# Fused top-k attention and two MoE layers on one core: keys and queries turned plain and stacked by DMA, last two batches in two visits

## Chip, cores and metric

The kernel runs on one core of a Trainium2 chip. The time is device time in microseconds (us) of the whole program, from inputs in HBM to outputs in HBM. The engines are PE (TensorE), VectorE (DVE), ScalarE (ACT), GpSimd (POOL) and SP, which in this kernel issues the DMAs.

## What is computed

Three layers follow each other; the output of one is the input of the next.

```python
# attention: B, H, S, D = 4, 8, 576, 64
scores = q @ k.T / 8
kth = np.partition(scores, -32, axis=-1)[..., -32:-31]
attn = softmax(where(scores >= kth, scores, -1e9))
x = (attn @ v)                      # -> 2304 tokens x 512
# first MoE
x = ((x @ w1) * (x @ w2)) @ w3 @ w_out
# second MoE: 8 experts, w1 512 x 1024, w2 1024 x 512
P = exp(x @ w_gate - max); 8 times: divide by row sums, by column sums, scale
out = sum over e of P[:, e:e+1] * (maximum(x @ w1[e], 0) @ w2[e])
```

## The kernel before

**Attention.** A *visit* is one batch and one pair of heads (`visits`, line 92). Two visits make a group of nine *steps* (`steps1`, line 220): four steps with 128 query rows of both heads of the first visit, one step for the 64 rows that are left over of both visits, four steps of the second visit. There are 72 steps. In a step `st_scores` multiplies queries with keys (L251), `st_topk` finds the 32nd largest score on VectorE with rounds of max and replace (L300, L305), `st_over`, `st_exp` and `st_norm` make the weights, `st_trans` turns them (L360, L361) and `st_av` multiplies them with the values (L389). Three steps are in work at once: scores for step s + 1, top-k of s, weights of s - 1, values of s - 2. A string in `ORDERS` (three of them: for steps below `SWITCH`, for the other steps with weight conversion, and for the rest) tells in which order a step's pieces are issued: S scores, T the maxima that feed top-k, f and d top-k, O and E weights, N normalising, R turning, A values, P a piece of preparation, C a weight conversion, F filling, X handing over a batch.

Scores have fp32 accuracy from two fp32r halves: a key is kept as high and low half, stacked over 128 partitions, and in a second tile with the halves swapped (`kst[p, 0]`, `kst[p, 1]`); queries are stacked likewise in `qst_t`. `prep_list(p)` makes these for visit p: `prep_split` (ScalarE copies the high half, GpSimd subtracts), `prep_group` (PE turns blocks of both halves side by side, L174, ScalarE copies them out, L133), and `prep_swap` (two DMAs make the swapped tile, L207). The loop over p (from L745) spreads these pieces over steps. `load_pair` and `load_v` fetch keys, queries and values; all DMAs are issued by SP, in the order of the program.

**First MoE.** While batch 0 is in attention, weights are converted (`convert`, `cv_run`) and w3 @ w_out is folded into `W` (L538). A batch's products become *filling* when its last step is done (`pdone`, `marks`): `moe1_list` gives, for a part of 256 or 320 tokens, `x_split`, 32 pieces of `ab` (six matmuls each, L588) and 16 of `x2_mm` (L606), and the gate's logits (`gate_parts`, `gate_sums`). `run_fill` takes pieces of it from the list `fill` up to a budget `per`, which deals what is left evenly over the steps to the last mark. The last batch's filling runs after attention.

**Second MoE.** Three thirds of the tokens, eight experts, four pieces of the hidden layer make 96 *units*. `l1` multiplies x with the first weights in seven products (L1005), `l2` multiplies the result with the second (L1066) and adds it up on VectorE (L1079). Seven places a unit call `slot()`, which takes one entry of the list `steps`: x of the next third is loaded, summed (VectorE, L921), and split (ScalarE L924, GpSimd L927) there by `x_ops`. `w_split` and `w2_split` split weights on ScalarE and GpSimd (L893, L894, L901, L902).

Of the kernel before, what the change touches and what calls it, by code (L numbers as in the profile page):

```python
# [7 lines left out]
F32 = mybir.dt.float32  # L8
# [10 lines left out]
def kernel(  # L19
# [45 lines left out]
    nc.sync.dma_start(wg[:, :, 0:E], w_gate.rearrange("(c p) e -> p c e", p=128))  # L65
# [25 lines left out]
    SPLIT = {}  # L91
# [15 lines left out]

    def load_pair(p):
        b, hp, (t0, t1), tail = visits[p]
        for nm, src, r0, r1, end in (("k", k, 0, R, True), ("q", q, t0, t1, tail)):  # L110
            t = ap1.tile([128, 2 * R + 1, D], F32, name=f"{nm}n", tag=f"{nm}n", bufs=1)
            nc.sync.dma_start(
                t[:, 0:2 * R].rearrange("p (h r) d -> p h (r d)", h=2)[:, :, D * r0:D * r1],
                src[b, 2 * hp:2 * hp + 2, 0:S4, :].rearrange("h (p r) d -> p h (r d)", r=R)[:, :, D * r0:D * r1])
            for i in range(2 if end else 0):
                nc.sync.dma_start(t[64 * i:64 * i + 64, 2 * R], src[b, 2 * hp + i, S4:S, :])
            nat[nm, p] = t

# [18 lines left out]
    def prep_split(p, nm, eng=nc.gpsimd, three=False):  # L137
        src = nat.pop((nm, p))
        if three:
            hl = xT[0].rearrange("p c s -> p (c s)")[:, 0:3 * S].rearrange("p (n a d) -> p n a d", a=3, d=D).bitcast(F32R)  # L140
        else:
            hl = ap1.tile([128, 2 * R + 1, 2, D], F32R, name=f"{nm}hl", tag=f"{nm}hl")
        (t0, t1), tail = visits[p][2:]
        if nm == "k" or t1 - t0 == R:
            parts = [(src, hl[:, :, 0, :], hl[:, :, 1, :])]
        else:
            hr = hl[:, 0:2 * R].rearrange("p (h r) a d -> p h r a d", h=2)[:, :, t0:t1]
            parts = [(src[:, 0:2 * R].rearrange("p (h r) d -> p h r d", h=2)[:, :, t0:t1], hr[:, :, :, 0], hr[:, :, :, 1])]
            if tail:
                parts.append((src[:, 2 * R], hl[:, 2 * R, 0], hl[:, 2 * R, 1]))  # L150
        for x, hi, lo in parts:
            nc.scalar.activation(hi, x, AF.Copy)
            eng.tensor_tensor(lo, x, hi.bitcast(F32), ALU.subtract)
        if three:
            nc.scalar.activation(hl[:, :, 2, :], src, AF.Copy)
        split[nm, p] = hl

    def qgroups(p):
        (t0, t1), tail = visits[p][2:]
        n = t1 - t0  # L160
        heads = [[R * h + t for t in range(t0, t1)] for h in range(2)]
        r = heads if n > 2 else [heads[0] + heads[1]]
        if tail:
            r = r[:-1] + [r[-1] + [2 * R]] if n == 1 else r + [[2 * R]]
        return r

    def prep_group(p, nm, g, eng=None, flip=False):
# [22 lines left out]
        else:  # L190
            n = int(flip)
            if (p, n) not in kst:
                kst[p, n] = ap1.tile([128, 2, S], F32R, name=f"kst{n}", tag=f"kst{n}", bufs=2)
# [8 lines left out]
    def prep_swap(p, hs=slice(0, 2), ts=slice(0, S)):  # L202

        if (p, 1) not in kst:
            kst[p, 1] = ap1.tile([128, 2, S], F32R, name="kst1", tag="kst1", bufs=2)
        for i in range(2):
            nc.sync.dma_start(kst[p, 1][64 * i:64 * i + 64, hs, ts].bitcast(F32),  # L207
                              kst[p, 0][64 - 64 * i:128 - 64 * i, hs, ts].bitcast(F32))

    def prep_list(p):  # L210
        ops = [lambda: prep_split(p, "k"), lambda: prep_split(p, "q")]
        for nm in ("k", "q"):
            for g in kgroups if nm == "k" else qgroups(p):
                ops.append(lambda nm=nm, g=g: prep_group(p, nm, g))
            if nm == "k":
                ops.append(lambda: prep_swap(p))
        return ops
# [129 lines left out]
    def st_eps(st):  # L347
        nc.gpsimd.tensor_scalar(rden[st], rden[st], 1e-9, None, op0=ALU.add)
# [125 lines left out]
    def cv_list():  # L474
# [14 lines left out]
        def add3(i, hf):  # L489
            add(("3", i, hf), w3[128 * i:128 * i + 128, CW * hf:CW * hf + CW], lambda: w3dst(i, hf),  # L490
                lambda: later(4, w_items(i, hf)))
# [67 lines left out]
    def x_split(b, hf):  # L559
# [4 lines left out]
        eng, step = (nc.vector, 1) if b == B - 1 else (nc.gpsimd, KD)  # L564
# [8 lines left out]
    def ab(b, hf, f, which, part):  # L573
# [7 lines left out]
        for c in (2 * part, 2 * part + 1):  # L581
# [5 lines left out]
            for j, (lhs, rhs) in enumerate(((wh, xh), (wh, xl), (wl, xh))):  # L587
                nc.tensor.matmul(ps[:, 0:n], lhs, rhs[:, c, 0:n],  # L588
                                 start=(c == 0 and j == 0), stop=(c == KD - 1 and j == 2))
# [40 lines left out]
    def gate_sums(b, hf):  # L630
# [548 lines left out]
```

## Time and profile before

| | us |
|---|---|
| median of 3 runs | 2362.26 (2357.11 to 2362.8) |
| the profiled execution, its own time | 2360.21 |
| its span in the profile | 2358.4 |
| PE busy | 2257.2 (96%) |
| VectorE busy | 1874.8 (79%) |
| GpSimd busy | 1563.2 (66%) |
| ScalarE busy | 1262.4 (54%) |

The span is what the profile shows from the first instruction to the last; the 1.8 us around it belong to the time. PE's busy time counts matmuls that overlap, so a busy PE need not be full. Engines are busy by turns, so the shares have to be read by stage. In the profile's names L251 is line 251 of the kernel, and `kst<-pt` is an instruction that reads tile pt and writes kst.

### The profile page before, as it was taken

How to read it: one execution, taken by the hardware profiler on the slowest of the kernel's cores; microseconds unless marked ns; L12 is line 12 of the kernel's file. 1: busy time of each engine (PE TensorE's matmuls, PEld its weight loads, DVE VectorE, ACT ScalarE, POOL GpSimd, SP SyncE). 2: the span in 40 equal slices, each digit the busy share in tenths (PEclk: the TensorE clock that was granted, in tenths of full speed). 3: DMA queues.
4: the chain of work that ended last, by engine and by line, in shares of the span. 5: the costliest groups of instructions: out<-in, count | busy, mean ns of one | idle time of the engine just before them, and what ended most of it. 6: DMA issues, size and time to landing. Idle time of an engine off the chain costs nothing.

```text
span 2358.4 us, 38935 instructions
## 1 busy us (share of the span) xinstructions
PE 2257.2 (96%) x13108; PEld 1990.3 (84%) x13108; DVE 1874.8 (79%) x4352; ACT 1262.4 (54%) x2763; POOL 1563.2 (66%) x1727
## 2 busy tenths in 40 slices
PE   4797899999999999999999999999999999999999
PEld 4554888897997989899999988899998999999998
DVE  7899999999994378887777777777777677777776
ACT  7899788787874344443343453344434434344432
POOL 5789876776763156866666677666666666666664
PEclk7898899999999999999999999999999999999999
DMA  4433111111101022222222232222222222222221
GB/s 149 125 115 116 26 46 53 34 43 53 31 21 44 29 69 85 76 70 66 72 64 72 86 94 68 67 67 68 71 65 68 94 72 63 72 63 72 68 67 54
DMA packets 171704, 161.34 MB, mean 68 GB/s; under 512 B 21360, under 2 KB 136048, under 8 KB 171504
## 3 DMA queue, kind: packets, MB, share of 16 engines
q1 hardware_dynamic: 171504, 158.86, 22.8%
q8 instruction: 103, 1.69, 0.3%
q14 instruction: 97, 0.79, 0.1%
HBM read 140.53 MB, written 9.44 MB: 64 GB/s over the span
## 4 chain that ended last, share of the span: by engine, by line
PE 83%; DVE 5%; ACT 5%; POOL 4%; issue 1%; DMA 1%; SPq 0%; POOLq 0%; ACTq 0%; DVEq 0%
PE y L1066 33%; PE l1ps L1005 29%; PE abps L588 8%; PE x2ps L606 4%; PE sps L251 3%; PE tx L389 2%; PE tx L360 2%; DVE tkv L300 2%; DVE rest L305 1%; PE pt L174 1%; ACT s_sb L341 1%; ACT et L363 1%; POOL xl L568 1%; PE wps L538 1%; ACT xT L446 0%
## 5 line engine op out<-in xcount | busy, mean ns | idle before, releaser
L894 POOL TENSOR_TENSOR wal<-ws,wah 128x256 fp32r<-128x256 f32 x665 | 546.6, 830 | 476.3 <-ACT wah L893 468.7
L1079 DVE SCALAR_TENSOR_TENSOR acc<-y,P,acc 128x512 f32<-128x512 f32 x540 | 402.3, 745 | 205.2 <-PE y L1066 203.5
L893 ACT ACTIVATE wah<-ws 128x256 fp32r<-128x256 f32 x672 | 276.7, 413 | 516.4 <-PE l1ps L1005 510.9
L1066 PE MATMUL y<-wbh,hh 128*128 128x512 f32 x1152 | 454.3, 394 | 5.4 <-ACT hh L1026 5.3
L1066 PE MATMUL y<-wbl,hh 128*128 128x512 f32 x1152 | 455.5, 395 | 0.0
L1066 PE MATMUL y<-wbh,hl 128*128 128x512 f32 x1152 | 452.6, 393 | 1.6 <-DVE hl L1029 1.2
L887 DVE TENSOR_TENSOR ws<-ws 128x256 f32<-128x256 f32 x384 | 327.7, 854 | 0.1
L1005 PE MATMUL l1ps<-xo0h,wah 128*128 128x384 f32 x896 | 303.1, 338 | 0.0
L1005 PE MATMUL l1ps<-xo0l,wah 128*128 128x384 f32 x896 | 301.6, 337 | 0.0
L1005 PE MATMUL l1ps<-xo0h,wal 128*128 128x384 f32 x896 | 301.4, 336 | 0.0
L1026 ACT ACTIVATE hh<-u 128x384 fp32r<-128x384 f32 x192 | 100.9, 526 | 296.9 <-DVE u L1018 296.9
L1066 PEld LDWEIGHTS y<-wbl,hh 128*128 128x128 f32 x1152 | 216.8, 188 | 48.9
L1066 PEld LDWEIGHTS y<-wbh,hh 128*128 128x128 f32 x1152 | 216.8, 188 | 32.3 <-ACT hh L1026 7.7
L1066 PEld LDWEIGHTS y<-wbh,hl 128*128 128x128 f32 x1152 | 216.9, 188 | 30.0 <-DVE hl L1029 4.8
L902 POOL TENSOR_TENSOR wbl<-ws,wbh 128x1024 fp32r<-128x1024 f32 x96 | 232.0, 2416 | 11.9 <-ACT wbh L901 2.8
L277 POOL TENSOR_TENSOR low<-s_sb 128x288 int32<-128x288 int32 x144 | 118.9, 825 | 111.5 <-ACT s_sb L255 108.9
L1005 PEld LDWEIGHTS l1ps<-xo0l,wah 128*128 128x128 f32 x896 | 168.6, 188 | 17.1
L1005 PEld LDWEIGHTS l1ps<-xo0h,wah 128*128 128x128 f32 x896 | 168.4, 188 | 14.5
L300 DVE MAX8 tkv<-rest 128x8 f32<-128x288 f32 x432 | 174.7, 445 | 0.0
L1005 PEld LDWEIGHTS l1ps<-xo0h,wal 128*128 128x128 f32 x896 | 168.4, 188 | 0.0
L1018 DVE TENSOR_TENSOR u<-l1ps,u 128x384 f32<-128x384 f32 x288 | 157.0, 545 | 4.3 <-PE l1ps L1005 2.5
L251 PE MATMUL sps<-kst,qst 128*128 128x288 f32 x640 | 132.7, 336 | 28.5 <-DVE top L284 28.4
(166 smaller groups left out, 5219.8 us busy)
## 6 DMA issues: line engine op xcount, KB each, us to landing
ws<-in_moe_w_dram SPq DMA_DIRECT2D x384, 128.0 KB, 2.3
ws<-in_moe_w_dram SPq DMA_DIRECT2D x96, 512.0 KB, 3.5
raw<-in_moe_w_dram SPq DMA_DIRECT2D x32, 512.0 KB, 3.9
kst<-kst SPq DMA_DIRECT2D x30, 288.0 KB, 4.1
xr<-x2s SPq DMA_DIRECT2D x12, 384.0 KB, 3.8
kn<-in_k_dram SPq DMA_DIRECT2D x16, 256.0 KB, 3.2
qn<-in_q_dram SPq DMA_DIRECT2D x16, 256.0 KB, 3.0
raw<-in_moe_w_out_dram SPq DMA_DIRECT2D x8, 512.0 KB, 4.3
```

Source lines behind the costliest of these rows:

```text
L251: nc.tensor.matmul(ps[:, e, 0:SH], lhs, kst[p, part][:, hh, SH * e:SH * e + SH], start=(n == 0), stop=(n == len(terms) - 1))
L277: nc.gpsimd.tensor_tensor(low_sb[st][:, j].bitcast(I32), x[:, 0:SH], x[:, SH:S], ALU.add)
L300: nc.vector.max(vt[:, j, c:c + 8], x[:, j])
L588: nc.tensor.matmul(ps[:, 0:n], lhs, rhs[:, c, 0:n], start=(c == 0 and j == 0), stop=(c == KD - 1 and j == 2))
L887: nc.vector.tensor_tensor(st[:, dst], st[:, x], st[:, y], op)
L893: nc.scalar.activation(hi, st[:, slot], AF.Copy)
L894: eng.tensor_tensor(lo, st[:, slot], hi.bitcast(F32), ALU.subtract)
L902: nc.gpsimd.tensor_tensor(lo, st, hi.bitcast(F32), ALU.subtract)
L1005: nc.tensor.matmul(ps[:, 0:TH], lhs[:, c], rhs[:, slot, c], start=(k_ == 0), stop=(k_ == 3 * KH - 1))
L1018: nc.vector.tensor_tensor(t[nm], ps, t[x], ALU.add)
L1066: nc.tensor.matmul(ps, lhs[:, m, h, o:o + 128], rhs[:, m], start=(k_ == 0), stop=(k_ == 5))
L1079: nc.vector.scalar_tensor_tensor(a, ps, P[:, t, e:e + 1], a, op0=ALU.mult, op1=ALU.add)
```

## The change

- **Preparation of keys and queries.** They are loaded so that both heads' 64 columns lie side by side, turned once in fp32 (`prep_turn`, four transposes; the left-over rows of keys and queries share one, `prep_ends`), copied out by ScalarE, split after that (`prep_parts`, ScalarE and GpSimd), and the halves are stacked into `kst` and `qst_t` by six and four to eight DMAs (`prep_stack`). The old three functions are gone but for the first visit.
- **Two visits for the last two batches.** `SPLIT` makes each pair of heads of batches 2 and 3 come twice, first with query rows 0 to 255, then with the rest; keys are loaded and prepared for both. There are 24 visits for 16; the number of steps stays 72. A batch's first 256 tokens become filling after its first four visits.
- **Dealing.** `per` is also held to what lasts until the next mark.
- **First loads.** `load_first` puts the first queries on ScalarE's queue, `split_first` splits in pieces, the gate's weights are loaded later, the first scores come before the second head is prepared.
- **Issue orders** in `ORDERS`; one more conversion may wait (`len(dve_q) > 3`), w3's products come two ticks later; `x_split` works in chunks of two; the first product piece reads low halves last; the gate's copies wait in `held`.
- **Second MoE.** The first two products of the first unit (`first_ps`) are issued before the last gate piece. For later thirds, x's four sums take a place each, and places 3 and 4 of a unit call no `slot()` from the seventh unit on.

```diff
-    SPLIT = {}
+    SPLIT = {B - 2: 2, B - 1: 2}
...
+    def prep_turn(p, nm):
+        src = nat.pop((nm, p))
...
+        for t in range(c0 // 128, c1 // 128):
+            nc.tensor.transpose(pt[:, 128 * t:128 * t + 128], src[:, t].rearrange("p h d -> p (h d)"), ident)
+        copy(flat_x[nm, p].bitcast(F32)[:, 1, c0:c1], pt[:, c0:c1], None, scale if nm == "q" else 1.0)
...
+    def prep_parts(p, nm):
...
+        nc.scalar.activation(hi, lo.bitcast(F32), AF.Copy)
+        nc.gpsimd.tensor_tensor(lo, lo.bitcast(F32), hi.bitcast(F32), ALU.subtract)
+
+    def prep_stack(p, nm):
...
+            for h in range(2):
+                x = hl[64 * h:64 * h + 64]
+                nc.sync.dma_start(ks.bitcast(F32)[0:64, :, h], x)
+                for a in range(2):
+                    nc.sync.dma_start(ks.bitcast(F32)[64:128, 1 - a, h], x[:, a])
+            return
+        for h in range(2):
+            for a in range(2):
...
+                nc.sync.dma_start(d[:, S4 * h + c0:S4 * h + cb], x[:, c0:cb])
+                if c1 == S:
+                    nc.sync.dma_start(d[:, 2 * S4 + 192 * h:2 * S4 + 192 * h + 64], x[:, S4:S])
...
-        eng, step = (nc.vector, 1) if b == B - 1 else (nc.gpsimd, KD)
+        eng, step = (nc.vector, 1) if b == B - 1 else (nc.gpsimd, 2)
...
-        "X C N F f0 O0 S0 d0 P f1 d1 T0 R0 O1 B F R1 f2 d2 f3 L F g0 C C P F P C C E0 F V e0 F E1 Q g1 S1 A C F F J T1",
+        "F f0 N P S0 C d0 R0 X P O0 f1 d1 T0 F O1 B R1 F L f2 d2 f3 g0 C C P E0 F C F V C P C F S1 e0 E1 g1 Q C J T1 A F",
...
+            have = todo[0] - sum(work[m] for m in marks[:-1] if m >= s)
+            for m in marks[:-1]:
+                if m >= s:
+                    per = min(per, have / (m + 1.5 - s) / 4)
+                    have += work[m]
...
-            steps += [lambda c=c: sums(c), None]
             if s == 0:
+                steps += [lambda c=c: sums(c), None]
...
+                steps += [lambda c=c, n=n: sums(c, n) for n in range(4)] + [None]
...
+        if len(fill) == 1:
+            for x in order[:2]:
+                first_ps[x] = l1_prod(0, 0, 0, x)
...
-            slot()
+            if n < 6 or i not in (3, 4):
+                slot()
```

Three places show what moves. The first is PE's order from the last weighted values of attention on; abps is the first MoE's first product, x2ps its second, lgps the gate. Before:

```order
L361 MATMUL tx<-ident,s_sb 128x128
L389 MATMUL tx<-et,vn_96 64x128 x10
L606 MATMUL x2ps<-G,W 128x320 x4
L588 MATMUL abps<-xh,w1h 128x256
L588 MATMUL abps<-xl,w1h 128x256
L588 MATMUL abps<-xh,w1l 128x256
L588 MATMUL abps<-xh,w1h 128x256
L588 MATMUL abps<-xl,w1h 128x256
L588 MATMUL abps<-xh,w1l 128x256
L625 MATMUL lgps<-x2st,wg 32x320 x4
```

and with the change:

```order
L398 MATMUL tx<-ident,s_sb 128x128
L426 MATMUL tx<-et,vn_95 64x128 x10
L644 MATMUL x2ps<-G,W 128x256 x8
L627 MATMUL abps<-xh,w1h 128x320 x4
L627 MATMUL abps<-xh,w1l 128x320 x2
L663 MATMUL lgps<-x2st,wg 32x256 x4
L627 MATMUL abps<-xh,w1l 128x320 x2
L627 MATMUL abps<-xl,w1h 128x320 x4
L674 MATMUL lgps<-fold,x2st 128x8 x2
```

Before, both parts of the last batch stand behind this place, the 256-column one first; now it is the 320-column part alone.

The second is SP's order in batch 2, where a visit is half as long as before; vn are values, ends the left-over rows, x2s the first MoE's result. Before:

```order
L207 DMA kst_4904<-kst_4743 64x1152 x2
L613 DMA x2s<-x2st 128x256
L615 DMA x2s<-x2st 128x64
L123 DMA vn_96<-in_v_dram 128x256 x2
L126 DMA vn_96<-in_v_dram 64x64 x2
L112 DMA kn<-in_k_dram 128x2x256
L116 DMA kn<-in_k_dram 64x64 x2
L112 DMA qn<-in_q_dram 128x2x256
L116 DMA qn<-in_q_dram 64x64 x2
L207 DMA kst_5607<-kst_5377 64x1152 x2
```

and with the change, for one visit with query rows 0 to 255:

```order
L134 DMA vn_94<-in_v_dram 128x256 x2
L137 DMA vn_94<-in_v_dram 64x64 x2
L248 DMA qst_97<-qt 64x256 x4
L124 DMA kn<-in_k_dram 128x4x64 x2
L126 DMA ends<-in_k_dram 64x2x64
L124 DMA qn<-in_q_dram 128x2x64 x2
L126 DMA ends<-in_q_dram 64x2x64
L240 DMA kst<-kt 64x2x576
L242 DMA kst<-kt 64x576 x2
L240 DMA kst<-kt 64x2x576
L242 DMA kst<-kt 64x576 x2
L134 DMA vn_95<-in_v_dram 128x256 x2
```

One pair of swap copies between two visits' loads has become six copies of keys and four of queries; the queries' copies stand behind the next load of values.

The third is GpSimd's order in the second MoE while x of the next third is prepared; wbl is the split of the second weights, xo1l the low half of x, u and p sums that the hidden layer waits for. Before:

```order
L1023 TENSOR_TENSOR u_11596<-u_11572,p_11549 128x384
L894 TENSOR_TENSOR wal_11607<-ws_11360,wah_11606 128x256
L902 TENSOR_TENSOR wbl<-ws_11437,wbh 128x1024
L927 TENSOR_TENSOR xo1l<-xr,xo1h 128x384
L894 TENSOR_TENSOR wal_11639<-ws_11360,wah_11638 128x256
L927 TENSOR_TENSOR xo1l<-xr,xo1h 128x384
L1023 TENSOR_TENSOR p_11549<-u_11626,p_11549 128x384
L894 TENSOR_TENSOR wal_11663<-ws_11360,wah_11662 128x256
L894 TENSOR_TENSOR wal_11693<-ws_11360,wah_11692 128x256
```

and with the change:

```order
L1084 TENSOR_TENSOR u_12061<-u_12037,p_12014 128x384
L948 TENSOR_TENSOR wal_12072<-ws_11830,wah_12071 128x256
L956 TENSOR_TENSOR wbl<-ws_11906,wbh 128x1024
L948 TENSOR_TENSOR wal_12102<-ws_11830,wah_12101 128x256
L1084 TENSOR_TENSOR p_12014<-u_12089,p_12014 128x384
L948 TENSOR_TENSOR wal_12124<-ws_11830,wah_12123 128x256
L982 TENSOR_TENSOR xo1l<-xr,xo1h 128x384
L948 TENSOR_TENSOR wal_12153<-ws_11830,wah_12152 128x256
L982 TENSOR_TENSOR xo1l<-xr,xo1h 128x384
```

Two low halves of x stood between the split of the second weights and p; now none does.

## Rows read from the trace of the kernel before

**Rows 1.** Busy time by stretch: busy us (instructions) of PE, PEld, DVE, ACT, POOL; PEclk, DMA, GB/s.

```profile
63.30:248.70 185.40, 148.47 (x920) 100.36 (x921) 170.72 (x562) 175.37 (x358) 153.53 (x181) 0.90 0.37 112
248.70:414.50 165.80, 161.72 (x1338) 146.04 (x1339) 159.78 (x597) 132.56 (x298) 119.02 (x172) 0.97 0.16 43
414.50:721.60 307.10, 299.06 (x2507) 269.43 (x2505) 293.94 (x1097) 241.60 (x540) 215.28 (x312) 0.98 0.13 35
...
745.60:834.50 88.90, 87.75 (x553) 78.09 (x553) 20.72 (x39) 26.87 (x61) 15.31 (x17) 1.00 0.16 46
...
1009.70:1337.30 327.60, 327.60 (x1640) 295.59 (x1639) 258.90 (x402) 132.32 (x294) 213.57 (x210) 1.00 0.23 68
```

**Rows 2.** Chain of waits, attention steps paced by VectorE: start us, us, what.

```profile
700.17 1.44 DVE tkv L300 x4
...
709.02 1.44 DVE tkv L300 x4
```

**Rows 3.** Chain of waits, one attention step from 352.29 to 361.14.

```profile
352.29 1.24 PE tx L389 x20
353.53 0.73 PE sps L251 x4
...
355.13 0.44 PE pt L174 x4
...
356.44 0.44 PE tx L360 x4
...
357.87 0.53 PE sps L251 x4
...
361.14 1.24 PE tx L389 x20
```

**Rows 4.** Chain of waits, from the end of attention to the second MoE.

```profile
749.40 21.79 PE abps L588 x180
...
785.01 0.87 PE abps L588 x6
...
787.87 26.50 PE abps L588 x180
814.37 17.23 PE x2ps L606 x64
...
834.53 2.28 PE l1ps L1005 x12
```

**Rows 5.** ScalarE by line and shape, 63.3 to 248.7 us: count | busy us, mean ns | idle before.

```profile
L133 ACT ACTIVATE kst<-pt 128x512 fp32r<-128x512 f32 x8 | 4.8, 603 | 0.4 <-PE pt L174 0.4
...
L152 ACT ACTIVATE khl<-kn 128x576 fp32r<-128x576 f32 x3 | 2.1, 706 | 0.0
...
L133 ACT ACTIVATE kst<-pt 128x128 fp32r<-128x128 f32 x4 | 1.2, 288 | 0.0
...
L133 ACT ACTIVATE qst<-pt 128x64 fp32r<-128x64 f32 x6 | 1.0, 222 | 0.5 <-PE pt L174 0.5
```

**Rows 6.** DMA issues of the whole run: count, KB each, median us to landing.

```profile
kst<-kst SPq DMA_DIRECT2D x30, 288.0 KB, 4.1
```

**Rows 7.** Instructions of ScalarE in order of time, first 10 us.

```profile
5.76 0.68 ACT L152 ACTIVATE xT<-kn 128x576 fp32r<-128x576 f32 x1 [2.99 <-DMA kn<-in_k_dram]
```

**Rows 8.** Chain of waits, second MoE: first product of units 7, 9, 32 and 38.

```profile
942.03 2.10 PE l1ps L1005 x12
...
977.78 2.09 PE l1ps L1005 x12
...
1337.31 2.09 PE l1ps L1005 x12
...
1438.04 2.10 PE l1ps L1005 x12
```

**Rows 9.** Instructions of ScalarE in order of time, second MoE, from 955 us.

```profile
962.13 0.52 ACT L1026 ACTIVATE hh<-p 128x384 fp32r<-128x384 f32 x1 [6.04 <-POOL p L1023]
```

**Rows 10.** Waits of SP's queue: who waited for whom: us in total, times, longest.

```profile
SPq L123 <- PE tx L377: 71.2, 10, 14.4
```

More of the change, by code (lines that the diff above doesn't have):

```diff
@@ L135, in copy, with split_first @@
             eng.tensor_copy(dst, src)
[L137 to L140, printed above, removed]
-        else:
[L142 to L165, printed above, removed]
+    def split_first(nm, c, eng=nc.vector):
+        src = nat[nm, 0]
+        if nm == "k":
+            hl = xT[0].rearrange("p c s -> p (c s)")[:, 0:3 * S].rearrange("p (n a d) -> p n a d", a=3, d=D)
+        else:
+            hl = W.rearrange("p f d -> p (f d)")[:, 3 * DM:3 * DM + 2 * S].rearrange("p (n a d) -> p n a d", a=2, d=D)
+        hl = hl.bitcast(F32R)
+        nc.scalar.activation(hl[:, c, 0, :], src[:, c], AF.Copy)
+        eng.tensor_tensor(hl[:, c, 1, :], src[:, c], hl[:, c, 0, :].bitcast(F32), ALU.subtract)
+        if nm == "k":
+            nc.scalar.activation(hl[:, c, 2, :], src[:, c], AF.Copy)
+        split[nm, 0] = hl
     def prep_group(p, nm, g, eng=None, flip=False):
@@ L192, in prep_group @@
             if (p, n) not in kst:
[L193 removed]
+                ks = ap1.tile([128, 2, 2, S], F32R, name="kst", tag="kst", bufs=2)
+                for m in range(2):
+                    kst[p, m] = ks[:, m]
             dst = kst[p, n]
@@ L200 @@
     kgroups = [list(range(R)), list(range(R, 2 * R)), [2 * R]]
[L202 to L208, printed above, removed]
-    def prep_list(p):
[L211 to L217, printed above, removed]
+    flat_x = {}
@@ new lines, in prep_ends @@
+    def prep_ends(p):
+        src = nat.pop(("e", p)).rearrange("p h d -> p (h d)")
+        pt = mps.tile([128, 512], F32, name="pt", tag="mm")
+        rows = {"k": slice(0, SR), "q": slice(64, 64 + SR)}
+        if not visits[p][3]:
+            rows.pop("q")
+        nc.tensor.transpose(pt[:, 0:128], src, ident)
+        for nm, r in rows.items():
+            copy(flat_x[nm, p].bitcast(F32)[:, 1, S4:S], pt[:, r], None, scale if nm == "q" else 1.0)
+    def prep_parts(p, nm):
+        c0, c1 = cols_of(p, nm)
+        hi, lo = [flat_x[nm, p][:, a, c0:c1] for a in range(2)]
+        nc.scalar.activation(hi, lo.bitcast(F32), AF.Copy)
+        nc.gpsimd.tensor_tensor(lo, lo.bitcast(F32), hi.bitcast(F32), ALU.subtract)
@@ L580, in ab @@
         fs = slice(128 * f, 128 * f + 128)
-        for c in (2 * part, 2 * part + 1):
+        kinds = [(c, j) for j in (0, 2, 1) for c in range(KD)] if f == 0 and not which else [
+            (c, j) for c in range(KD) for j in range(3)]
+        for m, (c, j) in list(enumerate(kinds))[6 * part:6 * part + 6]:
             if which:
@@ L688 @@
     credit = [0.0]
+    held = []
     def run_fill(budget):
         credit[0] += budget
+        while held:
+            held.pop(0)()
         while fill and credit[0] > 0 and fill[0][1] is not None:
@@ L764 @@
     marks = sorted(pdone)
-    todo = [sum(c for s in marks[:-1] for c, _ in moe1_list(*pdone[s]))]
+    work = {s: sum(c for c, _ in moe1_list(*pdone[s])) for s in marks[:-1]}
+    todo = [sum(work.values())]
     gates.clear()
     ORDERS = (
[3 rows of a table removed]
[3 rows of a table added]
     )
@@ L988, with l1_prod @@
     hs = {}
+    first_ps = {}
+    def l1_prod(s, e, u, slot):
+        xh, xl = xo[s % 2]
+        ps = lps.tile([128, 512], F32, name="l1ps", tag="l1")
+        ah, al = wts[e, u, "a", slot]
+        k_ = 0
+        for c in range(KH):
+            for lhs, rhs in ((ah, xh), (ah, xl), (al, xh)):
+                nc.tensor.matmul(ps[:, 0:TH], lhs[:, c], rhs[:, slot, c],
+                                 start=(k_ == 0), stop=(k_ == 3 * KH - 1))
+                k_ += 1
+        return ps[:, 0:TH]
     def l1(s, e, u):
-        xh, xl = xo[s % 2]
         t = {}
```

118 lines of the change are left out of this document (74 added, 44 removed), and 4 rows, old and new, of the table ORDERS.

## The prediction

> **What bounds the kernel now.** I read the page first, then busy time by stretch, then the chain of waits inside single steps. The program has four stages: start and attention with weight conversion (to 248.7 us), attention with the first MoE as filling (to 745.6), the rest of the first MoE alone (to 834.5), the second MoE (to the end). In the first of them ScalarE is nearly full: 175 of 185 us between 63.3 and 248.7 [rows 1]. From 248.7 on PE and VectorE are both over 95% busy until 721.6 [rows 1], so it has to be seen which ends a step. A step is one round of top-k: without other trouble VectorE's rounds start 8.85 us apart [rows 2]. The chain inside one such step, from 352.29 to 361.14, is nothing but PE, without a gap [rows 3]: the step lasts 8.85 us on PE as well. The reader is to see there that the attention steps have almost no room for more matmuls. From 745.6 to 834.5 PE works alone on the last batch's first MoE while VectorE is idle three quarters of the time [rows 1, 4]. In the second MoE a unit takes 15.60 us (21 units in the 327.6 us of [rows 1]); losses stand out against that.
>
> **Last two batches in two visits.** Before, the last batch's products all wait for attention to end: the 256-column part from 745.6 to 785.0, the 320-column part from there to 834.5 [rows 4]. Now batch 3's first 256 queries are finished at step 61 of 72, and their products become filling. So the end loses 785.0 - 745.6 = 39.4 us; some 1 us of this comes back, because eight matmuls of the part before (before: four) are left over when attention ends: **-38.5**. The last gate takes 834.53 - 814.37 - 17.23 = 2.93 us [rows 4], a third of it, as I estimate, waits, which the second MoE's first two products now fill (12 matmuls, 2.28 us [rows 4]): **-1**. The inputs that the second MoE prepares in this stretch take VectorE 20.7 us [rows 1]; in the 50 us that are left they still fit.
>
> What moves into attention is not free. The dealing holds batch 0's products to what lasts until batch 1 comes, so steps 20 to 37 stay at VectorE's pace: 18 x 8.85 = 159.3, with the first step's wait for the split some 163.3, against 165.8 before [rows 1, 2]: **-2.5**. Steps 38 to 70 then carry the rest. The prices: a product matmul of 256 columns 0.121 us (21.79/180), of 320 columns 0.147 (26.50/180); the second product 13.8 us a part of 256 (785.01 - 749.40 - 21.79) and 17.2 a part of 320 [rows 4]. A part costs 192 x 0.121 + 13.8 = 37.0 or 192 x 0.147 + 17.2 = 45.5, with some 0.9 each for the gate's matmuls in the same chain. Batches 1 and 2, the first part of 3 and what is left of batch 0 (8 us), less what stands behind step 70 (20 us; both counted in the new order at these prices), are 193 us, or 5.85 a step. The rest of a step on PE [rows 3]: 1.24 for the weighted values, 0.73 + 0.53 for scores, 2 x (0.44 + 0.11) for transposes, together 3.60; 0.15 for the tail steps' second set of scores (4 in 33); and for preparing, 7 transposes a visit and a visit in 2.25 steps, 0.34 (0.44 for four [rows 3]). Sum 9.9 us, above VectorE's 8.85: PE sets these steps. 33 x 9.9 = 327 against 307.1 [rows 1]: **+20**. Its bounds: 0, if PE's idle pieces take all of it, and +35, if each of the 16 visits also costs a wait of 1 us.
>
> Here a rule speaks the other way. The Trainium skill (Perfetto Trace Analysis, Identifying the Most-Contended Engine) says that matmul busy time is a bad measure of PE's room and that the weight loads' busy share is a good one. By it 269.4 of 307.1 us are taken [rows 1], 12% or 37 us are free, and the moved part would fit without lengthening anything. I go by the chain, in which a step is full at 8.85 us; the other reading is a rival below.
>
> **Keys and queries turned plain.** Before, a pair is split into high and low halves, 18 transposes, and copied out of PSUM by ScalarE; now it is turned once (9 transposes, or 7 in a half visit), split after, and stacked by DMA. 279 + 18 transposes become 175 + 27, though keys are prepared 23 times and not 16; 95 x 0.11 = 10 us of PE, which the sums above hold where PE counts. On ScalarE a key costs before 0.706 + 2 x 0.603 + 0.288 = 2.20, now 0.603 + 0.222 + 0.706 = 1.53 [rows 5]; a query, priced alike with its two short copies, 2.36 and 1.53. That is 1.5 us a pair, and 3.5 pairs fall into the stretch to 248.7 in which ScalarE is full: **-5**. Later ScalarE has room and nothing is gained. The new issue orders and the looser limit on conversions act in the same stretch; nothing shows their worth alone. Its VectorE is busy 170.7 of 185.4 us [rows 1], so at best some 9 us more go, and a bad place costs as much; the nearest row, ScalarE's 10 idle us, says little can go, so I take 0, with -9 and +13 for the range.
>
> The price of it is SP's queue: 793 issues become 1132. A pair's stack is six copies for keys and four to eight for queries, behind loads that wait for a free place. The nearest row is the swap that they replace, 4.1 us to landing [rows 6]. They are issued one step ahead of the scores, and I count them as hidden by that step; without it, see the last rival.
>
> **First loads.** ScalarE's first split waits 2.99 us for keys, queries' copies and tails issued in one queue, and starts at 5.76 [rows 7]. Now keys come first, each piece is split alone, and the first scores need one head. Between nothing and 2.5 us, I take **-1.5**.
>
> **Places for the second MoE's x.** Units 7 and 8 take 35.75 us (942.03 to 977.78), and the six from 1337.31 to 1438.04 100.73, against 31.2 and 93.6: 11.7 us lost [rows 8]. In the first of them ScalarE stands 6.04 us for GpSimd's p [rows 9], which is behind the second weights' split and two low halves of x. The change puts no x work behind these, and spreads VectorE's four sums over four places. I take **-9**; bounds -11.7 and -3, since x takes six units now instead of three to four.
>
> **Sum.** -1.5 - 5 - 2.5 + 20 - 38.5 - 1 - 9 = -37.5 against the profiled execution's 2360.2: 2322.7. That execution is 2.1 us under the median of the runs, so I name **2325 us**. The small edits (the gate's copies held back, a multiply by one more, later weight products) I cost at nothing: they ride on engines with room, and would cost their own fractions of a us.
>
> **Rivals.**
> *The moved part fits* (the skill's reading): steps 38 to 70 keep 307 us, and the sum is -57.5: 2305 us. For it stands that 307.1 us are 15 more than 33 steps of 8.85, so PE does wait somewhere [rows 1, 2]; against it the chain without a gap [rows 3]. Chance 0.12.
>
> *The first stage gives back.* The way of a key now runs transpose, copy, split, DMA, and conversion loads stand behind the copies in SP's queue. With 1 us more in each of the first 20 steps, and the 5 us not gained, the time is 2350. For it: ScalarE and VectorE are both over 92% busy there, so any order that waits costs at once. Against: the pairs are turned four steps ahead. Chance 0.17.
>
> *The stacks come late, and the kernel gets slower.* In half visits a query's stack is emitted two steps before its step, behind the load of values, and the scores go one step before. SP has stood up to 14.4 us at such a load, 71.2 us at ten of them [rows 10]; before, only swaps and loads with time were behind it. PE works in order, so a stack that lands after the scores' turn stops PE and with it everything. The time is above 2362 from 1.7 us a visit on (37.5/22), and 2.0 us a visit, 44 in all, give 2369. Against it: from emission two parts of work of under 1.5 us, eight issues and a landing of 4.1 us are some 9 us, and a step of 9.9 lies between. The Trainium skill (DMA: Bandwidth & Descriptors, Specifications) says that runs under 512 bytes are written by read-modify-write, which the loads of keys and queries in runs of 64 floats would meet; no row shows it for copies of this size. With that I give it 0.06 instead of 0.04.
>
> **Chances and range.** The forecast has 0.65; with its terms' bounds it runs from 2309 to 2341. The range takes in the rival that fits at one end and most of the first stage's at the other: 2305 to 2347. About 0.3%, 7 us, is what the measurement can tell from no change: faster than 2355 come the forecast, the fitting rival and three quarters of the first stage's, 0.90; the rest is shared, 0.05 within and 0.05 slower.
>
> **What would show it.** From attention's last step to the second MoE's first product some 50 us instead of 89; steps 38 to 70 near 9.9 us apart, with a chain that is PE throughout; no long step where one batch's products run out; ScalarE's busy time before 248.7 some 5 us down; units 7, 8 and 33 to 38 near 15.6 us. Waits of PE's scores for a DMA would show the slow rival, and steps of 8.9 us after step 38 the fitting one. I am wrong if the time is outside the range, or if the gain lies in another stage than the end of attention.

## The result, and the profile after

The changed kernel takes 2330.1 us (median of 4 runs, 2329.79 to 2331.99) against 2361.12 of the kernel before beside it: a ratio of 0.9873, 95% interval 0.9858 to 0.9887. The forecast was 2325 (2305 to 2347), faster. The profiled executions have spans of 2358.4 and 2328.0 us. By stage, cut at the starts of top-k rounds (VectorE's first instruction of a round) and at the second MoE's first product, in us:

| stage | before | after | difference | predicted |
|---|---|---|---|---|
| start to the first round | 16.2 | 14.8 | -1.4 | -1.5 |
| steps 0 to 19 | 232.5 | 223.5 | -9.0 | -5 |
| steps 20 to 37 | 165.8 | 164.5 | -1.3 | -2.5 |
| steps 38 to 70 | 307.1 | 332.6 | +25.5 | +20 |
| step 71 and the end of the first MoE | 112.9 | 77.3 | -35.6 | -38.5, -1 |
| second MoE | 1523.9 | 1515.3 | -8.6 | -9 |

Every term has its sign; the sum is 7 us short, 5.5 of them in steps 38 to 70 and 3.9 at the end, with 4 regained in steps 0 to 19. Busy time of the changed kernel in these stages (steps 1 to 9, 10 to 19, 20 to 37, 38 to 70, end), columns as in [rows 1]:

```profile
25.80:124.90 99.10, 74.62 (x454) 51.11 (x454) 96.59 (x316) 92.01 (x187) 77.89 (x97) 0.86 0.62 165
124.90:238.30 113.40, 88.09 (x522) 58.97 (x522) 107.21 (x351) 104.52 (x213) 102.29 (x118) 0.85 0.44 120
238.30:402.80 164.50, 158.00 (x1296) 140.83 (x1297) 159.53 (x596) 127.55 (x288) 117.99 (x173) 0.98 0.30 71
402.80:735.40 332.60, 328.16 (x2703) 296.43 (x2704) 298.45 (x1103) 256.12 (x586) 233.65 (x338) 1.00 0.43 101
735.40:812.70 77.30, 74.03 (x477) 62.54 (x477) 29.28 (x66) 30.22 (x65) 18.48 (x23) 0.98 0.16 48
```

The fourth row is the one to read. PE is busy 328.2 of 332.6 us where it was 299.1 of 307.1 [rows 1], and VectorE, busy 293.9 of 307.1 us before, now has 34 us free. A step's chain from one weighted-values piece (L426) to the next is PE's work alone, and takes 10.08 us:

```profile
481.60 1.24 PE tx L426 x20
482.84 0.72 PE sps L288 x4
...
491.68 1.24 PE tx L426 x20
```

Over the whole stretch the chain is not PE throughout. Its shares by line, as far as the view prints them:

```profile
by line: PE abps L627 32.3%; PE x2ps L644 13.6%; PE sps L288 11.4%; PE tx L426 8.3%; PE tx L397 7.2%; DMA kst<-kt 3.2%; issue 2.7%; SPq L242 2.6%; PE pt L211 2.0%; PE tx L398 1.8%; SPq L240 1.4%; POOL kt L228 1.3%; DMA qst<-qt 1.2%; PE tx L
```

Some 77% of it is PE by these lines; some 10% is the splitting and stacking of keys and queries (POOL kt, SPq L240 and L242, the two DMAs).

For steps 1 to 9 and 10 to 19 the kernel before has:

```profile
28.80:135.70 106.90, 79.86 (x468) 56.32 (x468) 97.45 (x316) 94.45 (x191) 75.89 (x96) 0.82 0.38 115
135.70:248.70 113.00, 86.84 (x553) 59.65 (x554) 104.93 (x352) 109.46 (x224) 101.83 (x116) 0.89 0.36 107
```

Steps 1 to 9 lost 7.8 us, but ScalarE's busy time only 2.4 of them. What went is VectorE's idle time, 9.5 to 2.5 us: before, it waited for GpSimd and ScalarE. VectorE's waits there, before (who waited for whom: us in total, times, longest):

```profile
DVE tkv L300 <- POOL low L289: 4.0, 4, 2.0
DVE rden L317 <- POOL rden L348: 1.7, 1, 1.7
DVE top L284 <- ACT s_sb L255: 1.2, 1, 1.2
```

After, these are 0.3 us in all. In steps 10 to 19 it is the other way round: ScalarE has 4.9 us less to do and nothing is won.

The chain of waits of the changed kernel from the end of attention to the second MoE, and two units of it:

```profile
758.97 4.04 PE x2ps L644 x16
...
764.00 1.78 PE abps L627 x6
...
766.35 1.07 PE abps L627 x6
...
767.76 26.50 PE abps L627 x180
794.26 17.23 PE x2ps L644 x64
811.49 1.25 PE lgps L663 x8
812.74 2.29 PE l1ps L1055 x12
...
937.82 2.08 PE l1ps L1055 x12
...
953.42 2.08 PE l1ps L1055 x12
```

The 256-column part's 21.8 and 13.8 us [rows 4] are gone from here. What is left of it when attention ends is 16 matmuls (4.04 us), and from there to the long row at 767.76 8.8 us pass. Before, the 320-column part got to its long row in 2.9 us, from 785.0 to 787.87 [rows 4]. A unit of the second MoE is 15.60 us (953.42 - 937.82) where units 7 and 8 took 35.75 together [rows 8]. ScalarE no longer stands 6.04 us for GpSimd's p [rows 9]; the like instruction now, in order of time, has no wait behind it:

```profile
961.49 0.51 ACT L1087 ACTIVATE hh<-p 128x384 fp32r<-128x384 f32 x1
```

Unit 0 takes 11.5 us instead of 9.5. With 10.6 us regained after it, that makes the stage's 8.6.

Waits of the changed kernel in steps 38 to 70, PE's and ScalarE's:

```profile
PE lgps L663 <- ACT kt L144: 1.5, 1, 1.5
PE sps L288 <- DMA qst<-qt: 1.1, 2, 0.7
...
ACT kt L144 <- DMA kst<-kt: 7.9, 5, 4.0
```

PE's other four kinds of wait there are 2.0 us together. PE's scores hardly wait for a stack. ScalarE does: the next visit's turned keys go into the one buffer that the stack before still reads.

### The profile page after: what moved, and what is told of

Read it like the earlier page. It is cut to its first block, busy times and chain, and to the rows that moved or that the text cites. A ratio compares the mean times of both kernels' runs of the same rounds, so it can differ in the third digit from the quotient of the medians.

```text
span 2328.0 us, 39531 instructions
## 1 busy us (share of the span) xinstructions
PE 2239.2 (96%) x13013; PEld 1972.1 (85%) x13013; DVE 1881.1 (81%) x4356; ACT 1257.2 (54%) x2770; POOL 1583.2 (68%) x1749
## 4 chain that ended last, share of the span: by engine, by line
PE 79%; DVE 9%; ACT 4%; POOL 4%; DMA 2%; issue 2%; SPq 1%; ACTq 0%; POOLq 0%; DVEq 0%
PE y L1127 33%; PE l1ps L1055 29%; PE abps L627 6%; PE x2ps L644 3%; DVE tkv L337 3%; PE sps L288 2%; DVE rest L342 2%; PE tx L426 2%; PE tx L397 2%; POOL low L326 1%; DVE low L342 1%; ACT s_sb L378 1%; DMA kst<-kt 1%; DVE top L321 1%; DVE ws L941 1%
## 5 line engine op out<-in xcount | busy, mean ns | idle before, releaser
L941 DVE TENSOR_TENSOR ws<-ws 128x256 f32<-128x256 f32 x384 | 322.6, 841 | 0.7 <-POOL u L1084 0.4
L1055 PEld LDWEIGHTS l1ps<-xo0h,wah 128*128 128x128 f32 x896 | 168.0, 188 | 14.8 <-issue 0.5
```

The costliest lines, as they stand in the source:

```text
L941: nc.vector.tensor_tensor(st[:, dst], st[:, x], st[:, y], op)
L1055: nc.tensor.matmul(ps[:, 0:TH], lhs[:, c], rhs[:, slot, c], start=(k_ == 0), stop=(k_ == 3 * KH - 1))
```

## Experiments

Theory: from step 38 on PE sets the steps, so moved products cost nearly what they weigh; the new preparation pays by the work it takes from PE and ScalarE; the 5.5 us too many in these steps are waits for late stacks. Rivals: PE had room (the reading by weight loads); the long steps come from the stacks by DMA and not from the products; in steps 0 to 19 it is the orders alone that gain. Stages of every run in us (0-9 are steps 0 to 9; ratio to the kernel before measured beside the run, 95% interval):

| run | 0-9 | 10-19 | 20-37 | 38-70 | end | second MoE | median | ratio |
|---|---|---|---|---|---|---|---|---|
| before | 119.5 | 113.0 | 165.8 | 307.1 | 112.9 | 1523.9 | 2361.1 | 1 |
| after | 110.1 | 113.4 | 164.5 | 332.6 | 77.3 | 1515.3 | 2330.1 | 0.9873 (0.9858-0.9887) |
| e1 | 110.2 | 113.1 | 164.2 | 300.3 | 113.4 | 1515.2 | 2334.8 | 0.9902 (0.9888-0.9915) |
| e2 | 110.9 | 113.3 | 164.3 | 330.0 | 81.0 | 1514.7 | 2329.4 | 0.9881 (0.9868-0.9895) |
| e3 | 119.2 | 113.0 | 165.2 | 350.1 | 79.9 | 1524.0 | 2368.0 | 1.0047 (1.0033-1.0060) |
| e4 | 110.2 | 113.3 | 169.7 | 419.1 | 77.4 | 1515.2 | 2424.2 | 1.0286 (1.0272-1.0300) |
| e5 | 111.4 | 127.0 | 163.8 | 365.7 | 76.8 | 1516.6 | 2381.8 | 1.0098 (1.0083-1.0113) |
| e6 | 118.7 | 102.5 | 187.1 | 325.0 | 116.4 | 1522.8 | 2388.7 | 1.0127 (1.0112-1.0142) |
| e7 | 110.8 | 113.5 | 164.4 | 334.6 | 75.8 | 1514.9 | 2333.2 | 0.9894 (0.9878-0.9911) |
| e8 | 110.1 | 113.5 | 165.8 | 333.7 | 79.3 | 1516.0 | 2336.7 | 0.9906 (0.9891-0.9921) |
| e9 | 110.9 | 113.3 | 164.5 | 352.2 | 76.0 | 1514.9 | 2349.5 | 0.9957 (0.9941-0.9974) |
| e10 | 111.0 | 113.4 | 164.3 | 312.1 | 111.7 | 1514.6 | 2345.0 | 0.9940 (0.9923-0.9958) |
| e11 | 110.1 | 113.3 | 175.4 | 333.9 | 78.9 | 1514.8 | 2341.3 | 0.9921 (0.9902-0.9940) |
| e12 | 110.9 | 113.2 | 163.3 | 334.4 | 77.4 | 1526.3 | 2342.7 | 0.9926 (0.9906-0.9946) |

**e1: the change without the visits.**

```diff
-    SPLIT = {B - 2: 2, B - 1: 2}
+    SPLIT = {}
```

> The changed kernel with every batch in one visit again; all else stays. Theory (PE sets the steps from 38 on, so moved products cost nearly what they weigh): the end takes 112 us again instead of 77, steps 38 to 70 come back from 332.6 to 300-307 us, and the visits are worth only 3 to 10 us: 2333 to 2340. Rival (the longer steps come from the new preparation by DMA, not from moved products): steps 38 to 70 stay above 320 and the time is above 2353. Rival (the end's 36 us are nearly all gain, the steps are long for another reason that stays): also above 2353.

Measured: 2334.8 us, steps 38 to 70 at 300.3. Busy time of these steps:

```profile
403.30:703.60 300.30, 292.63 (x2461) 261.75 (x2461) 293.05 (x1097) 233.69 (x526) 215.48 (x316) 1.00 0.26 62
```

The theory's numbers hold. The chain of these steps is now VectorE's top-k first of all:

```profile
by line: DVE tkv L337 33.1%; DVE rest L342 18.8%; DVE low L342 7.4%; PE abps L627 6.4%; DVE top L321 6.2%; PE sps L288 3.1%; POOL xl L605 2.7%; ACT s_sb L378 2.0%; POOL low L326 2.0%; DVE tkv L352 1.8%; issue 1.7%; POOL s_sb L391 1.5%; PE t
```

The visits add 35.5 us to PE's busy time here and 32.3 us to the steps, and take 36.1 from the end: 3.8 us of gain by the stages, 4.7 by the medians, 6.8 by the ratios. Most of the change's gain, 23 us against the kernel before of the same comparison (2357.6), is there without them.

**e2: two visits for the last batch only.**

```diff
-    SPLIT = {B - 2: 2, B - 1: 2}
+    SPLIT = {B - 1: 2}
```

> The changed kernel with two visits for the last batch alone, 20 visits instead of 24. Theory: PE still sets every step after 38, its work is less by four keys' turning (4 x 7 x 0.11 us = 3 us) and some waits for stacks go with four visits fewer: 2322 to 2328, the end as short as in the changed kernel. Rival (batch 2's products, which now come all at once after step 56, do not fit before the end, or leave steps 38 to 55 at VectorE's pace with PE idle): 2335 or more, with steps after 56 above 11 us.

Measured: 2329.4 us, just outside the theory's 2328 and the same as the change. Its steps 38 to 55 and 56 to 70, busy time:

```profile
404.20:566.90 162.70, 158.26 (x1318) 140.24 (x1318) 159.58 (x599) 128.06 (x290) 117.88 (x173) 1.00 0.31 74
566.90:734.20 167.30, 166.56 (x1339) 150.72 (x1339) 138.07 (x507) 121.68 (x275) 108.17 (x157) 1.00 0.36 86
```

The changed kernel's, for the same steps:

```profile
402.80:583.90 181.10, 179.42 (x1496) 162.76 (x1497) 161.85 (x601) 141.17 (x325) 130.27 (x188) 1.00 0.45 107
583.90:735.40 151.50, 148.74 (x1211) 133.66 (x1209) 136.61 (x504) 114.95 (x262) 103.38 (x151) 1.00 0.39 94
```

PE's busy time falls by 3.3 us (324.8 against 328.2), as 28 transposes fewer should give. Only 2.6 us of that arrive, since half of the rival holds: steps 38 to 55 run at VectorE's pace (159.6 us busy), with 4.4 us of PE idle, and the steps after them are 11.2 us long. The end gives 3.7 back. Batch 2's two visits are thus worth nothing that can be measured.

**e3: the visits and the dealing in the kernel before.**

```diff
-    SPLIT = {}
+    SPLIT = {B - 2: 2, B - 1: 2}
...
+            have = todo[0] - sum(work[m] for m in marks[:-1] if m >= s)
+            for m in marks[:-1]:
+                if m >= s:
+                    per = min(per, have / (m + 1.5 - s) / 4)
+                    have += work[m]
```

> The kernel before with the two visits and the new dealing and nothing else of the change. Theory: the end is 36 us shorter, steps 38 to 70 pay 5.85 us of products each and 13 or 14 transposes a visit instead of 7, so about 10.2 us a step, 337 us; the first stages and the second MoE stay as before: 2351 to 2357. Rival (with the old way ScalarE's copies out of PSUM, 4 us a visit, hold PE up): steps of 10.7 us or more and no gain, 2362 or above.

Measured: 2368.0 us, slower than before. Busy time of steps 38 to 70:

```profile
412.20:762.30 350.10, 340.22 (x2787) 305.31 (x2788) 300.59 (x1103) 267.59 (x611) 233.61 (x341) 1.00 0.23 60
```

The end is 33 us shorter (36 expected), but the steps pay 43. The outcome is the rival's, the mechanism is not: PE is busy 340.2 us, 12.1 more than in the change, some 10 of it for the old way's transposes (182 instead of 91, at 0.11 us); 9.9 us are idle (the change: 4.4), and the largest wait in them is for GpSimd's split, not for ScalarE's copies:

```profile
PE pt L174 <- POOL khl L153: 5.5, 5, 1.3
```

So with visits the new preparation, with its orders and the small edits beside it, is worth 17.5 us in these steps, and without them 6.8 (307.1 to 300.3, e1). Alone, the visits lose.

**e4: the half visits' keys are turned one step later.**

```diff
-                prep.setdefault(ready[p] + min(n, 1), []).append(fn)
+                prep.setdefault(ready[p] + (1 if p > 8 else min(n, 1)), []).append(fn)
...
-            loads.setdefault(ready[p - 1] + (1 if p > 2 else 2), []).append(lambda p=p: load_pair(p))
+            loads.setdefault(ready[p - 1] + (1 if 2 < p < 10 else 2), []).append(lambda p=p: load_pair(p))
```

> The changed kernel with the keys' turning of the half visits (and the loads behind it) one step later, so that the stack before has a step more to leave the one buffer of turned keys. Theory (the 6 us above 9.9 a step are ScalarE waiting for that buffer and PE waiting for ScalarE): steps 38 to 70 come down from 332.6 to 326-329, the time to 2324-2327. Rival (the stack itself is what is late: with its emission a part of a step later, PE's scores wait for its DMA): steps 38 to 70 are as long or longer, 2330 or above.

Measured: 2424.2 us, 94 more than the change; the rival, and far beyond its number. Busy time of steps 38 to 70:

```profile
409.00:828.10 419.10, 352.04 (x2711) 316.55 (x2709) 301.84 (x1103) 260.03 (x586) 234.27 (x340) 0.91 0.34 82
```

PE's waits in them:

```profile
PE sps L288 <- DMA qst<-qt: 64.4, 14, 8.0
```

A piece of the chain of waits at one visit (L124 and L126 load the next pair, L248 stacks queries):

```profile
598.74 0.59 SPq L124
...
599.89 0.95 SPq L126
...
601.59 2.01 DMA qst<-qt
...
603.85 1.30 PE sps L288 x4
```

This is the slow rival of the prediction, brought about by an edit from which I had expected a gain. The next pair's loads (L124, L126) now stand in SP's queue between the keys' stack and the queries' stack, the queries land after their turn, and PE stands at the scores. 64.4 us are this wait; PE's busy time is 23.9 us longer for nearly the same matmuls, at a mean granted clock of 0.91 instead of 1.00. Together they are 88.3 us, against 86.5 that the stage grew (other waits shrank a little). In the piece shown the four loads hold SP's queue until 600.9, and PE stands 3.98 us before its scores: the queries' stack has less time to spare than these issues take.

**e5: the change with the orders of before, and e6: the kernel before with the new orders.**

```diff
-        "F f0 N P S0 C d0 R0 X P O0 f1 d1 T0 F O1 B R1 F L f2 ...
+        "X C N F f0 O0 S0 d0 P f1 d1 T0 R0 O1 B F R1 f2 d2 f3 ...
```

This is the first of e5's three orders, cut after some twenty places; e6 puts the new ones in place of the old.

> The changed kernel with the three issue orders of the kernel before. Theory (of the 9 us that steps 0 to 19 lost, some 5 are ScalarE's shorter preparing and some 4 the orders): steps 0 to 19 take 227-230 us instead of 223.5, steps 38 to 70 some us more, since the orders are made for seven pieces of preparing instead of nine or ten: 2336 to 2345. Rival (the orders did nothing): 223-225 us in steps 0 to 19 and 2328-2333. Rival (the orders did it all): 232 us.

> The kernel before with the three new issue orders and nothing else. Theory: with the old preparation ScalarE stays full in steps 0 to 19, so the orders alone bring little: steps 0 to 19 at 229-233 us (before 232.5), the time 2353 to 2362. Rival (the orders are the gain of these steps): 224 us and 2350.

Measured: 2381.8 and 2388.7 us. Each half of what I had priced as separate edits makes the kernel slower than before (ratios 1.0098 and 1.0127), and only both together gain. e5 keeps the visits, so its steps 38 to 70 judge the preparation with visits; its steps 10 to 19 lie before any half visit. e5's busy time in steps 10 to 19 and 38 to 70:

```profile
126.70:253.70 127.00, 88.99 (x536) 59.40 (x536) 109.01 (x352) 107.84 (x215) 104.67 (x118) 0.87 0.38 110
...
417.50:783.20 365.70, 339.37 (x2716) 303.63 (x2713) 301.14 (x1103) 259.14 (x587) 234.05 (x339) 0.97 0.39 93
```

Its waits, VectorE's in the first and PE's in the second of these stretches:

```profile
DVE top L321 <- ACT s_sb L292: 17.4, 10, 4.0
...
PE sps L288 <- DMA qst<-qt: 17.0, 9, 3.3
```

In steps 0 to 9 the old orders cost next to nothing (111.4 against 110.1) and the new ones alone win as little (e6: 118.7 against 119.5): there the gain is not the orders'. It is the preparation's, as I take it; that the first loads, the looser limit on conversions and the later w3 products have no part in it is not shown, since no run parts them. In steps 10 to 19 VectorE waits 17.4 us for scores (the change: 0.2), and from step 38 on the stacks come too late, as in e4. e6 in steps 10 to 19 and 20 to 37:

```profile
133.90:236.40 102.50, 86.35 (x553) 59.13 (x553) 98.52 (x343) 91.94 (x192) 76.07 (x98) 0.92 0.28 83
...
236.40:423.50 187.10, 156.22 (x1157) 137.29 (x1159) 167.48 (x605) 147.78 (x317) 140.85 (x185) 0.81 0.18 51
```

Its short steps 10 to 19 are no gain: ScalarE does 192 instructions there instead of 224, and the conversion left over runs in steps 20 to 37, which take 21 us more for 181 matmuls less; steps 38 to 70 take 17.9 us more. My expectations for both looked at one stage and missed the next; none of the forms I had given fits.

**e7 and e8: issues taken from SP's queue.**

```diff
+                eng = nc.gpsimd if h and p >= 8 else nc.sync
-                nc.sync.dma_start(ks.bitcast(F32)[0:64, :, h], x)
+                eng.dma_start(ks.bitcast(F32)[0:64, :, h], x)
...
-        nc.sync.dma_start(x2s[c, :, S4 * b + t0:S4 * b + t0 + m], st[:, 0:m])
+        nc.scalar.dma_start(x2s[c, :, S4 * b + t0:S4 * b + t0 + m], st[:, 0:m])
```

The first three lines are e7's (its two inner copies likewise), the last two e8's (and the store of the tail).

> The changed kernel with the three key-stack copies of the second head, from the ninth visit on, issued from GpSimd's queue instead of SyncE's (GpSimd has just made what they copy, so it waits for nothing). Theory (the stacks of the half visits are late because SyncE's queue is full of issues of 0.4 to 0.9 us each, and ScalarE and PE wait for them): steps 38 to 70 come down by 3 to 6 us from 332.6, the time to 2324-2327. Rival (GpSimd pays for the issues and its parts of top-k come later): steps 38 to 70 up, 2333 or more.

> The changed kernel with the stores of the first MoE's result (26 in steps 38 to 70, 0.4 us each on SyncE) issued from ScalarE's queue, which has just written what they store. Theory (SyncE's queue delays the stacks): steps 38 to 70 down by 2 to 4 us, the time to 2326-2328. Rival (the delay is elsewhere, or ScalarE's issues cost it as much): no change, 2329-2331, or slower.

Measured: 2333.2 and 2336.7 us, steps 38 to 70 at 334.6 and 333.7: the rivals, and no gain. e7's key stacks in these steps (DMA issues: count, KB each, median us to landing):

```profile
kst<-kt SPq DMA_DIRECT2D x28, 144.0 KB, 5.5
kst<-kt POOLq DMA_DIRECT2D x14, 288.0 KB, 5.2
...
kst<-kt SPq DMA_DIRECT2D x13, 288.0 KB, 3.4
```

and the changed kernel's:

```profile
kst<-kt SPq DMA_DIRECT2D x28, 288.0 KB, 3.5
kst<-kt SPq DMA_DIRECT2D x56, 144.0 KB, 3.7
```

e7's waits there, ScalarE's and VectorE's:

```profile
ACT kt L144 <- DMA kst<-kt: 6.4, 5, 3.1
...
DVE tkv L338 <- POOL low L327: 15.7, 26, 1.8
```

With two queues all but SP's own 288-KB copies take 1.7 to 1.8 us longer from issue to landing, ScalarE still waits 6.4 us (the change: 7.9), and VectorE waits 15.7 us for GpSimd instead of 6.0. So e7 trades one wait for another and does not decide what late stacks cost. e8 is the cleaner test: ScalarE's wait is 4.2 us instead of 7.9 and PE's busy time the same 328.2, and the steps are no shorter. That wait lies beside other work for the most part.

**e9 and e10: more matmuls in steps 38 to 70.**

```diff
+            for _ in range(2 if m == 0 and 38 <= now[0] <= 70 else 0):
+                nc.tensor.matmul(ps[:, 0:n], lhs, rhs[:, c, 0:n], start=True, stop=True)
             nc.tensor.matmul(ps[:, 0:n], lhs, rhs[:, c, 0:n], start=(m == 0), stop=(m == 3 * KD - 1))
```

> The changed kernel with each first-layer product of the first MoE that is issued in steps 38 to 70 given two more matmuls (its first one three times over, the last of them counts, so the output stays): 160 more, 96 of 256 columns and 64 of 320, at 0.121 and 0.147 us 21 us of PE. Theory (PE sets these steps and has no room): steps 38 to 70 go from 332.6 to 350-357 us, the time to 2348-2355. Rival (the free 11% of the weight loads' busy time is room): no change, 2329-2334.

> The same two more matmuls a product in the kernel of e1, where every batch has one visit: 128 more, 64 of each width, 17 us of PE. Theory: there VectorE sets most steps (8.85 us) and PE has some 8 to 14 us left in steps 38 to 70, so 3 to 9 us come through: steps 38 to 70 from 300.3 to 303-309, the time 2338 to 2344. Rival (PE is full there too): 317 us and 2352. Rival (room for all of it): 300 us and 2335.

Measured: 2349.5 and 2345.0 us. Busy time of steps 38 to 70 in e9:

```profile
404.10:756.30 352.20, 348.67 (x2859) 317.24 (x2860) 299.43 (x1103) 259.23 (x586) 233.88 (x338) 1.00 0.40 96
```

And in e10:

```profile
404.40:716.50 312.10, 307.15 (x2578) 277.89 (x2578) 294.48 (x1097) 238.32 (x526) 216.22 (x316) 1.00 0.25 60
```

160 matmuls put 20.5 us on PE's busy time and 19.6 on the steps, as the theory said: in the change PE has no room. In the kernel without visits 14.5 us of matmuls lengthen the steps by 11.8, more than the 3 to 9 I expected and less than the 17 of a full PE: there were 7.7 us of idle PE (300.3 - 292.6), but only 2.7 of them could be used.

**e11: without the new dealing.** The five lines that e3 adds are taken out.

> The changed kernel without the limit that holds a batch's products to what lasts until the next batch comes. Theory (PE is paid for the same work wherever it stands, but in steps 20 to 37 VectorE sets the pace with 6 us of PE left over, and after 38 PE does): batch 0's products run out before step 38 and the steps behind them lose PE's time: steps 20 to 37 some 5 to 10 us longer, 38 to 70 about as much shorter, in sum 0 to +5: 2330 to 2335. Rival (the limit is worth more, because long steps come back where a batch ends): above 2337.

Measured: 2341.3 us, the rival. Busy time of about steps 20 to 31 and 32 to 37:

```profile
239.00:357.00 118.00, 115.92 (x950) 108.70 (x951) 106.21 (x393) 89.40 (x199) 81.48 (x119) 0.96 0.24 57
357.00:414.40 57.40, 46.96 (x351) 37.52 (x352) 54.05 (x203) 41.14 (x92) 36.37 (x55) 0.92 0.37 87
```

Batch 0's products are dealt too fast: PE is full at first and then idle for 10.4 us. Steps 20 to 37 take 10.9 us more, and 38 to 70 win nothing for it.

**e12: the old places for the second MoE's x.**

```diff
-                steps += [lambda c=c, n=n: sums(c, n) for n in range(4)] + [None]
+                steps += [lambda c=c: sums(c), None]
...
-            if n < 6 or i not in (3, 4):
-                slot()
+            slot()
```

> The changed kernel with the second MoE's work on x at the places of before: five places in every unit and the four sums in one. Theory: units 7 to 10 and 33 to 38 lose again what they lost before, 8.6 to 10.6 us in all: 2338 to 2341. Rival (those losses had come from what stood before the second MoE): 2330 to 2333.

Measured: 2342.7 us, somewhat above the theory's 2341, the second MoE 11.0 us longer, and ScalarE's wait is back (instructions in order of time):

```profile
944.40 0.52 ACT L1087 ACTIVATE hh<-p 128x384 fp32r<-128x384 f32 x1 [5.36 <-POOL p L1084]
```

None of these versions beats the change; e2 equals it with four visits fewer.

## Why the prediction was right, and where it was not

*What bounds the kernel.* That PE and not VectorE would set steps 38 to 70 was the step on which most hung, and it is shown: by a step's chain, which is PE's alone for 10.08 us (9.9 forecast), by e1 (products taken out) and by e9 (matmuls put in). The sign "a chain that is PE throughout" holds for such steps and not for the stretch. The rule of the Trainium skill (Perfetto Trace Analysis, Identifying the Most-Contended Engine), read by the weight loads, would have given 296.4 of 332.6 us of weight loads, 11% free, and e9's matmuls for nothing. They cost 19.6 us; the trace disagrees, and the rival that fits is out.

*Last two batches in two visits.* The end's term was -39.5 and measured -35.6: "some 1 us of this comes back" was mis-sized. Sixteen matmuls and a gate are left over and not eight matmuls: 8.8 us before the last part's long row, where the sum left room for 3.9 (the part's own 2.9 and the 1). The last gate's -1 came to nothing: 1.25 us stand before the second MoE's first product instead of 2.93, but the rest of the gate and waits for it (0.8 and 1.5 us; before, one of 1.0) now lie in unit 0, which takes 2.0 us more. The term for steps 38 to 70 was +20 and measured +25.5. Its PE work was nearly right (327 planned, 328.2 busy; its products add up to 194.5 us by its own prices, not 193). What the sum lacked is 4.4 us in which PE is idle. The profile names six kinds of wait for them, the largest 1.5 us for ScalarE behind a keys' stack and 1.1 us for queries' stacks; e8 shows that relieving SP's queue of the stores doesn't win them, and what each costs the steps stays open. Steps 20 to 37 gave 1.3 instead of 2.5, and only with the dealing, which I had not priced by itself (e11: 11 us).

*Keys and queries turned plain.* -5 to step 19 was measured as -9.0, but the mechanism was mis-placed, so that its nearness is partly luck. I counted ScalarE's time. That fell by 7.4 us in steps 1 to 19 (203.9 to 196.5), yet the gain lies wholly in steps 0 to 9, where VectorE's waits for GpSimd and ScalarE went, and not in 10 to 19, where ScalarE lost more work. "Later ScalarE has room and nothing is gained" looked at ScalarE alone: without visits steps 38 to 70 win 6.8 us (e1), where PE has 55 transposes and 6.4 us of work less. The prediction had these transposes only inside its +20.

*Issue orders at nothing.* This step failed as a step, though the sum did not show it. Orders and preparation are not two terms: with the new preparation the old orders cost some 50 us (e5), outside the -9 and +13 that I had given them, and the new orders in the old kernel cost some 30 (e6). The bound "at best some 9 us more go, and a bad place costs as much" was drawn for one stage; most of the cost came in others.

*First loads.* -1.4 in the profile, against -1.5, but that this agrees is chance: the start of the first round scatters, 14.8 to 16.2 us in three runs with the old loads (before, e3, e6), 14.8 to 15.8 in eleven with the new. The second round starts at 27.4 to 28.9 and at 25.5 to 26.9. The gain of about 2 us is real, but it lies in step 0, which I had counted elsewhere.

*Places for x.* -9, measured -8.6 for the stage and -10.6 without unit 0, and 11.0 when undone (e12).

*Rivals.* The first stage gave nothing back. The stacks came in time, but with little to spare: with the loads in front of the queries' stack (e4) the kernel is slower than before by just this mechanism, and with the old orders (e5) it is a large part of the loss (17.0 us of waits for it in steps 38 to 70; 13.6 us more are lost in steps 10 to 19 for other waits).

The total is thus right partly by errors that cancel: 9 us too good in steps 38 to 70 and at the end, 4 too bad in the first twenty. The working of the range has a gap: the terms' bounds, added, run from about 2292 to 2360, and how they became 2309 to 2341 is not said. By the prediction's own terms the visits were to bring 22 of 37.5 us; the same stages brought 11.4 of 30.4 (35.6 + 1.3 - 25.5), and 6.8 of these are there without visits (e1), so that the visits themselves are worth 4 to 7. The sign of being wrong, "if the gain lies in another stage than the end of attention", has thus come half true: the end is by far the largest cut, but most of it is paid back in steps 38 to 70. Most of the gain is the preparation with its orders and the edits beside it, and the places.

## What to carry to other kernels

Before work is moved into another stage as filling, add up that stage's own instructions on the engine that would take it; where its chain has no gap, moved work costs its full weight, and only the difference of the two places is won. A preparation and the hand-written order it runs in are one edit: price them together, over all stages, since work pushed out of one stage returns in the next. For each copy that feeds an engine working in order, ask by how much it is early; here four load issues put in front of it were too many.

## What the runs showed of the hardware

In e4's steps 38 to 70 waits cost PE twice. It stood 64.4 us in 14 waits of up to 8.0 us, and behind them it ran slower: in the 2.15 us after the wait that ends at 603.85 (the piece shown above) the granted clock was 0.50, the lower of its two levels of 2.4 and 1.2 GHz, and from 608 on 1.00 again. Busy time in these 2.15 us, columns as in [rows 1]:

```profile
603.85:606.00 2.15, 2.15 (x9) 2.13 (x10) 0.00 (x0) 0.65 (x1) 0.09 (x1) 0.50 0.38 107
```

Over the stretch the mean was 0.91, and nearly the same matmuls took 352.0 us instead of 328.2. In e6's steps 20 to 37, where PE waited 17.9 us for top-k, the mean was 0.81 (before: 0.97).

Issuing half of a stack from GpSimd's queue made most of its copies take longer from issue to landing (e7: 5.2 to 5.5 us instead of 3.5 to 3.7 with the same bytes). Whether that comes from two queues at a time or from GpSimd's queue itself, no run shows.
